# Small scale steps made assignable to GpSimd, and another order of all work, in a fused window-attention and gated-FFN kernel

## The chip, the core and the metric

The kernel runs on one core of one Trainium2 chip. The metric is the time of one execution in device microseconds (us). The engines are named as in the profile: PE (TensorE, with PEld for its weight loads), DVE (VectorE), ACT (ScalarE), POOL (GpSimd) and SP (SyncE, which here only issues DMAs).

## The reference

Window attention over 8 batches x 8 heads x 576 positions of head size 64, and then a gated feed-forward layer over the 4608 tokens:

```python
scores = q @ k.T / sqrt(64)                 # per batch and head
mask = (rel >= 0) & (rel < 64)              # rel = i - j: each row sees 64 keys
attn = softmax(where(mask, scores, -1e9))
x = (attn @ v) as 4608 x 512                # heads side by side
h = x @ w_in                                # 512 -> 2048
g = h * erf(softplus(h))
out = g @ w_out                             # 2048 -> 512
```

Inputs and output are float32; the two weight matrices arrive as float64.

## The kernel before

**Split numbers.** Every operand of a matrix product is split into two float16 parts, a high one and a rest, after scaling by a power of two; a product is then three float16 matmuls (high x high, high x rest, rest x high). So each tensor has a step that finds its peak, a short chain of scale steps on 128x1 to 128x4 values, a "high" step and a "rest" step.

**Attention** runs in 36 units of 128 tokens (u = 0..35). Per unit: peaks of q, k, v (`pk`), high and rest of q, k, v (`qh ql kh kl vh vl`), scores on PE (`s`), masked maximum on DVE (`m`), subtraction of the maximum (`f`), exponential on ACT (`e`), high and rest of the probabilities (`ec`, `r`), a transpose by DMA (`t`), the product with v on PE (`a`), and the division (`n`). Two units form a chunk of 256 tokens (c = 0..17). The result x of a chunk is split again (`xh`, `xl`) and transposed by DMA (`xt`, into tiles `xt`), two sets of which alternate.

**The weights** come in 16 pieces (`L:0` to `L:15`), are put together from float64 by integer steps (`d`, `c`, `o`), and get a scale per pair of pieces: `mb mx my` find the peak, `mc` gives the power of two and its inverse, `dg` puts the inverse on a diagonal matrix, `h` makes the high part and `lp le` or `l` the rest. `W`, `V`, `X` join the scales of pairs.

**The feed-forward part** runs in 36 passes: pass g takes half of the hidden features (g % 2) of one chunk (g // 2). The first four chunks use plain products (`mm`, 24 matmuls of 256 columns each; line 643), the others seven products of sums (`mw`, 24 matmuls of 128 columns; line 696), whose results are copied out of PSUM (`ew`) and added (`xw`). Then come softplus (`sp`), erf (`er`), the gate (`gt`), the high part (`gh`, tile gh) and the rest (`gl`, tile gl) for each half n of the pass, and the second product (`mA` with gh, 16 matmuls of 512 columns, `mB` with gl, 8; line 754). `fo` scales the result, `st` stores it. Softplus, erf and the exponential need different ACT tables, so each change between them loads one.

**What sets the order.** PLAN is a list of tokens `step:unit:part:engine`, where a, v or g as the last part puts the step on ACT, DVE or POOL. The program issues the steps in the list's order, and each engine runs its own steps in that order, whatever is ready. `wm:k:n` puts n matmuls without use on PE. Waits between engines follow from the tiles. Small helpers make the steps: `scaled` (lines 346 to 352) multiplies by a scale on the engine asked for, `narrow` (line 481 on ACT, 483 on DVE, 485 on POOL) converts, `inverse_pow2` (line 343) turns a power of two into its inverse, always on DVE.

```python
for tok in PLAN.split():
    name, *args = tok.split(":")
    HANDLERS[name](*(int(a) if a.isdigit() else a for a in args))
```

Of the kernel before, what the change touches and what calls it, by code (L numbers as in the profile page):

```python
# [19 lines left out]
W = 64  # L20
# [16 lines left out]
LOWEST = -3.0e38  # L37
EXP_BITS = 0x7F800000
# [204 lines left out]
def window_attention_gated_ffn(ctx, tc, q, k, v, w_in, w_out, masks, out):  # L243
# [98 lines left out]
    def inverse_pow2(dst, src, shift):  # L342
        nc.vector.tensor_scalar(dst.bitcast(I32), src.bitcast(I32), -1.0, float((254 + shift) * EXP_ONE),
                                op0=ALU.mult, op1=ALU.add)
# [221 lines left out]
    def pair_diag(j):  # L566
        nc.scalar.activation(diag[j % 2], unit, AF.Copy, scale=parts(2 * j)[1])
# [272 lines left out]
```

## Time and profile before

| | |
|---|---|
| time, median of 3 runs | 865.0 us (864.99 to 865.01) |
| the profiled execution's own time | 864.18 us |
| its span | 862.4 us |
| mean granted clock of PE | 0.992 |
| PE, PEld busy | 834.7 us (97%), 590.3 us (68%) |
| DVE, ACT, POOL busy | 713.8 us (83%), 648.3 us (75%), 315.3 us (37%) |
| ACT table loads | 115, 1283 ns each |

The span runs from the first to the last instruction; 1.8 us of the profiled execution lie around it. A matmul's busy time counts work without use (`wm`) like any other. Shares are means over the span, and the first 140 us look different from the rest.

### The profile page before, as it was taken

What the parts mean: (1) busy time and instruction counts of PE and PEld (TensorE: products, weight loads), DVE (VectorE), ACT (ScalarE), POOL (GpSimd) and SP (SyncE); (2) the same over time, 40 slices, a digit from 0 to 9 for tenths busy, and PEclk for the clock granted to TensorE, in tenths of its full rate; (3) what the DMA queues carried; (4) which work ended last, traced back from release to release, by engine and by line L of the source; (5) the groups of instructions that cost most, each with busy time, mean ns of one, the idle gap of its engine ahead of it and who ended that gap; (6) DMA issues with size and microseconds to landing.
All of it is one profiled execution on the core that took longest, in us unless ns stands there. A gap on an engine that the chain in (4) does not pass through costs nothing.

```text
span 862.4 us, 25961 instructions
## 1 busy us (share of the span) xinstructions
PE 834.7 (97%) x11042; PEld 590.3 (68%) x11042; DVE 713.8 (83%) x1587; ACT 648.3 (75%) x820; POOL 315.3 (37%) x272
## 2 busy tenths in 40 slices
PE   6889989999999999999999999999999999999997
PEld 4557666666667775967867768777777676776773
DVE  5989998999998889988888797988798989774342
ACT  5989999988976797888697686976676664644452
POOL 2325223332342443335164434633234464331110
PEclk8999999999999999999999999999999999999999
DMA  9976573444442474574646747545245362420000
GB/s 362 332 183 187 171 208 107 92 115 83 123 102 60 124 146 108 149 140 115 141 117 121 153 117 180 108 120 118 66 112 121 92 119 39 93 44 26 2 26 24
DMA packets 167236, 104.45 MB, mean 121 GB/s; under 512 B 139856, under 2 KB 144592, under 8 KB 167120
## 3 DMA queue, kind: packets, MB, share of 16 engines
q1 hardware_dynamic: 167120, 102.80, 47.9%
q8 instruction: 86, 1.41, 0.6%
q14 instruction: 30, 0.25, 0.1%
HBM read 54.72 MB, written 9.44 MB: 74 GB/s over the span
## 4 chain that ended last, share of the span: by engine, by line
PE 80%; ACT 8%; DVE 6%; DMA 4%; issue 1%; SPq 0%; ACTq 0%; DVEq 0%
PE o L754 40%; PE hp L696 29%; PE hp L643 5%; PE av L469 3%; PE s L434 2%; DMA w<-w_in 1%; DMA xt<-xs 1%; DVE sm L443 1%; ACT y L721 1%; ACT L725 1%; ACT y L725 1%; ACT h L481 1%; DMA stage<-w_out 1%; ACT L721 1%; PE o L589 1%
## 5 line engine op out<-in xcount | busy, mean ns | idle before, releaser
L754 PE MATMUL o<-w,gh 128*128 128x512 f16 x1152 | 260.5, 379 | 0.1
L754 PEld LDWEIGHTS <-gh 128*128 128x128 f16 x1152 | 109.5, 98 | 122.5 <-ACT gh L481 0.3
L696 PEld LDWEIGHTS <-w 128*128 128x128 f16 x2688 | 156.0, 98 | 15.3
L696 PE MATMUL hp<-xt,w 128*128 128x128 f16 x2688 | 164.3, 219 | 0.0
L754 PE MATMUL o<-w,gl 128*128 128x512 f16 x576 | 136.2, 379 | 0.0
L696 PE MATMUL hp<-xt,stage 128*128 128x128 f16 x2016 | 122.5, 219 | 1.1 <-DMA xt<-xs 0.8
L696 PEld LDWEIGHTS <-stage 128*128 128x128 f16 x2016 | 116.2, 98 | 10.7 <-issue 1.2
L721 ACT ACTIVATE y<-h,c 128x1024 f32<-128x1024 f32 x72 | 80.0, 1143 | 34.4 <-DVE h L483 33.9
L730 DVE SCALAR_TENSOR_TENSOR y<-h,cy,y 128x1024 f32<-128x1024 f32 x56 | 76.4, 1380 | 22.0 <-ACT y L725 21.5
L643 PE MATMUL hp<-xt,w 128*128 128x256 f16 x768 | 89.9, 276 | 3.6 <-DMA xt<-xs 1.8
L754 PEld LDWEIGHTS <-gl 128*128 128x128 f16 x576 | 53.3, 98 | 54.0 <-DVE gl L355 0.3
L481 ACT ACTIVATE h<-hp 128x512 f32<-128x512 f32 x88 | 51.4, 588 | 48.7 <-PE hp L696 42.6
L452 ACT ACTIVATE sm<-sm,shift,cde 128x512 f32<-128x512 f32 x72 | 57.3, 808 | 39.9 <-DVE sm L448 32.9
L643 PEld LDWEIGHTS <-w 128*128 128x128 f16 x768 | 74.5, 99 | 16.4 <-issue 4.9
L712 DVE TENSOR_TENSOR h<-hp,h 128x512 f32<-128x512 f32 x84 | 57.5, 685 | 33.1 <-PE hp L696 27.2
L725 ACT ACTIVATE y<-y 128x1024 f32<-128x1024 f32 x72 | 74.1, 1053 | 0.5
L448 POOL TENSOR_TENSOR sm<-sm,mx 128x512 f32<-128x512 f32 x37 | 47.5, 1290 | 61.7 <-DVE mx L443 61.5
L459 POOL TENSOR_TENSOR p<-sm,p 128x512 f16<-128x512 f32 x37 | 52.0, 1409 | 43.8 <-DVE p L483 30.2
L443 DVE CUSTOM_DVE_ANT_0 sm<-s,mask 128x128 f32<-128x128 f32 x288 | 65.2, 284 | 3.2 <-PE s L434 2.7
L744 POOL TENSOR_TENSOR gl<-y,gh 128x1024 f16<-128x1024 f32 x20 | 45.0, 2250 | 60.3 <-DVE gh L483 23.0
L721 ACT ACT_TABLE_LOAD x45 | 57.7, 1283 | 5.4 <-DVE gl L355 2.3
L483 DVE COPY h<-hp 128x512 f32<-128x512 f32 x56 | 38.3, 685 | 26.5 <-PE hp L696 24.4
(160 smaller groups left out, 1302.7 us busy)
## 6 DMA issues: line engine op xcount, KB each, us to landing
kr<-k_in SPq DMA_DIRECT2D x36, 384.0 KB, 3.5
qr<-q_in SPq DMA_DIRECT2D x36, 256.0 KB, 3.4
vr<-v_in SPq DMA_DIRECT2D x18, 512.0 KB, 4.2
out<-ob SPq DMA_DIRECT2D x36, 256.0 KB, 2.1
stage<-w_out SPq DMA_DIRECT2D x6, 1024.0 KB, 5.4
stage<-w_in SPq DMA_DIRECT2D x5, 1024.0 KB, 5.7
vs<-vs SPq DMA_DIRECT2D x36, 130.0 KB, 2.6
vr<-v_in SPq DMA_DIRECT2D x18, 256.0 KB, 3.1
```

Source lines behind the costliest of these rows:

```text
L443: nc.vector.tensor_tensor_reduce(smi(u, par)[:, j, :], sps[par][:, j, :], mask[:, var, :], 1.0, LOWEST, op0=ALU.add, op1=ALU.max, accum_ou ...
L448: eng_of(eng).tensor_tensor(s, s, m.unsqueeze(2).broadcast_to([P, HP, P]), op=ALU.subtract)
L452: nc.scalar.activation(s, s, AF.Exp, bias=shift14, scale=es)
L459: eng_of(eng).tensor_tensor(pp[1][u % 2][:, sl, :], smi(u, par), pp[0][u % 2][:, sl, :], op=ALU.subtract)
L481: nc.scalar.activation(dst, src, AF.Copy)
L643: nc.tensor.matmul(hps[pc % 2][:, f, :], w1[a][:, cc, fs], xt[b][c % 2][:, cc:cc + 5:4, :], start=(n == 0), stop=(n == 3 * NCC - 1))
L696: nc.tensor.matmul(dst, w, xt[b][c % 2][:, blk + cc, :], start=bool(first) and at + cc + a + b == 0, stop=at + cc + a == 3 * P + 2, skip_g ...
L712: nc.vector.tensor_tensor(dst, bank_of((1, 0, 1)[i]), dst, op=ALU.add)
L721: nc.scalar.activation(yat(g, n), at(hb, g, n), AF.Softplus, scale=st_c[g][:, n:n + 1])
L725: nc.scalar.activation(y, y, AF.Erf)
L730: nc.vector.scalar_tensor_tensor(y, at(hb, g, n), s, y, op0=ALU.mult, op1=ALU.mult)
L754: nc.tensor.matmul(ops[j], a[:, f, ts], w2[b][:, hf * GF + f, :], start=first and f == 0 and a is gh and b == 0, stop=last and f == GF - 1 ...
```

## The change

Four things change in the code. The short scale chains get an engine of their own in PLAN: the pair's inverse leaves `mc` and becomes `md`, two of the chunk's scale steps leave `pc` and become `pd`, and `W`, `V` and `X` take an engine. The diagonal `dg`, always on ACT before, takes an engine too. Maxima of two columns by `tensor_reduce` or `tensor_tensor` become one `tensor_scalar` (`larger`). And PLAN is another list: 2677 tokens in place of 2652, in another order, with other engines for many steps.

```diff
+HUGE = 2.0 ** 127
...
-    def inverse_pow2(dst, src, shift):
-        nc.vector.tensor_scalar(dst.bitcast(I32), src.bitcast(I32), -1.0, float((254 + shift) * EXP_ONE),
+    def inverse_pow2(dst, src, shift, eng="v"):
+        eng_of(eng).tensor_scalar(dst.bitcast(I32), src.bitcast(I32), -1.0, float((254 + shift) * EXP_ONE),
                                 op0=ALU.mult, op1=ALU.add)
...
     def chunk_scale(c):
         nc.vector.tensor_copy(cpw[c], call)
         inverse_pow2(csc[c], cpw[c], 14)
-        nc.vector.tensor_scalar(cde[c][:, 0:1], cpw[c][:, 2:3], 2.0 ** -14, None, op0=ALU.mult)
-        nc.vector.tensor_scalar(cde[c][:, 1:2], cpw[c][:, 0:1], cpw[c][:, 1:2], 2.0 ** -31, op0=ALU.mult, op1=ALU.mult)
+
+    def chunk_gain(c, eng):
+        e = eng_of(eng)
+        e.tensor_scalar(cde[c][:, 0:1], cpw[c][:, 2:3], 2.0 ** -14, 1.0, op0=ALU.mult, op1=ALU.mult)
+        e.tensor_scalar(cde[c][:, 1:2], cpw[c][:, 0:1], cpw[c][:, 1:2], 2.0 ** -31, op0=ALU.mult, op1=ALU.mult)
...
     def pair_scale(j):
-        kw, sw, i = (kw1, sw1, j) if j < 4 else (kw2, sw2, j - 4)
-        kw, sw = kw[:, i:i + 1], sw[:, i:i + 1]
-        exponent(kw, wall)
-        inverse_pow2(sw, kw, 12 if j < 4 else 14)
-
-    def pair_diag(j):
-        nc.scalar.activation(diag[j % 2], unit, AF.Copy, scale=parts(2 * j)[1])
+        exponent((kw1, kw2)[j // 4][:, j % 4:j % 4 + 1], wall)
+
+    def pair_gain(j, eng):
+        kw, sw = ((kw1, sw1), (kw2, sw2))[j // 4]
+        inverse_pow2(sw[:, j % 4:j % 4 + 1], kw[:, j % 4:j % 4 + 1], 14 if j // 4 else 12, eng)
+
+    def pair_diag(j, eng):
+        scaled(eng, diag[j % 2], unit, parts(2 * j)[1])
...
-    def w_in_scale(hf):
+    def larger(eng, dst, a, b):
+        eng_of(eng).tensor_scalar(dst, a, HUGE, b, op0=ALU.min, op1=ALU.max)
+
+    def w_in_scale(hf, eng):
         wm = wm1[:, hf:hf + 1]
-        nc.vector.tensor_reduce(wm, kw1[:, 2 * hf:2 * hf + 2], axis=AX.X, op=ALU.max)
-        inverse_pow2(isw[:, hf:hf + 1], wm, -10)
+        larger(eng, wm, kw1[:, 2 * hf:2 * hf + 1], kw1[:, 2 * hf + 1:2 * hf + 2])
+        inverse_pow2(isw[:, hf:hf + 1], wm, -10, eng)
...
```

PLAN is shown at three places by the order of the instructions on an engine (`hp_154` and `hp_155` are the two PSUM tiles of the products, `o_156` and `o_157` those of the result, other numbers tell buffers apart).

**POOL, from its first real work on** (`sw` is the pair's inverse, `tmp` the diagonal, `w_0` the high part of w_in, `c_88` and `cde` scales, `sm` the scores, `p_` probabilities). Before:

```order
L352 TENSOR_SCALAR w_0_136<-stage_148,sw_66 128x2x512
L352 TENSOR_SCALAR w_0_136<-stage_149,sw_66 128x2x512
L352 TENSOR_SCALAR w_0_136<-w_1_139,sw_66 128x2x512
L621 TENSOR_SCALAR c_88<-kw_65,cpw 128x2
L448 TENSOR_TENSOR sm_116<-sm_116,mx_92 128x512
```

and now:

```order
L354 TENSOR_SCALAR tmp<-tmp,sw_66 128x128
L354 TENSOR_SCALAR w_0_136<-stage_149,sw_66 128x2x512
L345 TENSOR_SCALAR sw_66<-kw_65 128x1
L354 TENSOR_SCALAR w_0_136<-w_1_139,sw_66 128x2x512
L354 TENSOR_SCALAR tmp<-tmp,sw_66 128x128
L405 TENSOR_SCALAR cde<-cpw 128x1
L406 TENSOR_SCALAR cde<-cpw 128x1
L453 TENSOR_TENSOR sm_116<-sm_116,mx_92 128x512
```

Two diagonals, the inverse of the second pair (L345) and the two chunk scales (L405, L406) have come to POOL, one high part has left it.

**PE, where chunk 2 begins** (`xt_1` is chunk 1's x, `xt_0` chunk 2's; `av` from `pt_1` is the attention product of unit 5, the last of chunk 2; `cmx` and `cdiag` belong to the scale of the next chunk). Before:

```order
L469 MATMUL av<-vs_115,pt_1_126 64x65
L643 LDWEIGHTS w_0_136
L643 MATMUL hp_155<-xt_1_133,w_0_136 128x256
...
L387 MATMUL av<-ident,cmx 128x128
L395 LDWEIGHTS ones
L395 MATMUL av<-cdiag,ones 128x3
L643 LDWEIGHTS w_0_136
L643 MATMUL hp_155<-xt_0_132,w_0_136 128x256
```

and now:

```order
L474 MATMUL av<-vs_115,pt_1_126 64x65
L652 LDWEIGHTS w_0_136
L652 MATMUL hp_155<-xt_1_133,w_0_136 128x256
...
L389 MATMUL av<-ident,cmx 128x128
L652 MATMUL hp_154<-xt_1_133,w_0_136 128x256
...
L397 MATMUL av<-cdiag,ones 128x3
L652 MATMUL hp_155<-xt_1_133,w_0_136 128x256
...
L439 MATMUL s_151<-ks_0_110,qs_0_106 64x128
...
L652 MATMUL hp_155<-xt_0_132,w_0_136 128x256
```

Between unit 5's last attention matmul and chunk 2's first product stood one plain product (24 matmuls); now three of them and the scores of unit 6 (48 small matmuls) stand there.

**ACT, the last passes** (`y` is softplus and erf in place, `h_141` pass 35's hidden values, `ob` the result). Before:

```order
L348 ACTIVATE ob_147<-o_157,sg 128x512
L721 ACT_TABLE_LOAD
L721 ACTIVATE y_143<-h_141,c_88 128x1024
L721 ACTIVATE y_144<-h_141,c_88 128x1024
L725 ACT_TABLE_LOAD
L725 ACTIVATE y_143<-y_143 128x1024
L725 ACTIVATE y_144<-y_144 128x1024
```

and now:

```order
L350 ACTIVATE ob_147<-o_157,sg 128x512
L730 ACT_TABLE_LOAD
L730 ACTIVATE y_143<-h_141,c_88 128x1024
L734 ACT_TABLE_LOAD
L734 ACTIVATE y_143<-y_143 128x1024
L730 ACT_TABLE_LOAD
L730 ACTIVATE y_144<-h_141,c_88 128x1024
L734 ACT_TABLE_LOAD
L734 ACTIVATE y_144<-y_144 128x1024
```

The halves of pass 35 go through softplus and erf one after the other, with four table loads in place of two. On PE, `mA:34:0` now stands ahead of the last two products of pass 35 (`mw:35:3`, `mw:35:4`), where it stood behind them; so three groups of line 754 (`mB:34:0`, `mA:34:1`, `mB:34:1`) in place of four lie between the last product and `mA:35:0`.

Over the whole program the same steps change engines like this (steps before, now): copies out of PSUM `ew` on ACT 62, 82 and on DVE 50, 30; peaks `pk` on ACT 60, 42 and on DVE 48, 66; `f` on POOL 37, 45; `gl` on POOL 20, 28; table loads in ACT's order 115, 131. The matmuls with use are the same in number; those without are 276 and now 275.

More of the change, by code (lines that the diff above doesn't have):

```diff
@@ L593, in low_out @@
         narrow(eng, parts(u)[3][:, a], ops[a])
-    def w_in_scale(hf):
+    def larger(eng, dst, a, b):
+        eng_of(eng).tensor_scalar(dst, a, HUGE, b, op0=ALU.min, op1=ALU.max)
+    def w_in_scale(hf, eng):
         wm = wm1[:, hf:hf + 1]
-        nc.vector.tensor_reduce(wm, kw1[:, 2 * hf:2 * hf + 2], axis=AX.X, op=ALU.max)
-        inverse_pow2(isw[:, hf:hf + 1], wm, -10)
-    def w_out_scale(hf):
-        m, r = pm[:, hf:hf + 1], pr[:, hf:hf + 1]
-        pair = slice(2 * hf, 2 * hf + 2)
-        nc.vector.tensor_reduce(m, kw2[:, pair], axis=AX.X, op=ALU.max)
-        inverse_pow2(r, m, 0)
-        nc.vector.tensor_scalar(rw2[:, pair], kw2[:, pair], r, None, op0=ALU.mult)
-        nc.vector.tensor_scalar(kwo[:, hf:hf + 1], m, 2.0 ** -4, None, op0=ALU.mult)
@@ L608, in joint_scale @@
-    def joint_scale():
-        m, r, w, iw, ko = (all1[:, i:i + 1] for i in range(5))
-        nc.vector.tensor_tensor(m, pm[:, 0:1], pm[:, 1:2], op=ALU.max)
-        nc.vector.tensor_tensor(w, wm1[:, 0:1], wm1[:, 1:2], op=ALU.max)
-        inverse_pow2(r, m, 0)
-        inverse_pow2(iw, w, -10)
-        nc.vector.tensor_scalar(all4, kw2, r, None, op0=ALU.mult)
-        nc.vector.tensor_scalar(ko, m, w, 2.0 ** -4, op0=ALU.mult, op1=ALU.mult)
-        nc.vector.tensor_tensor(st_y, kw1, all4, op=ALU.mult)
-        nc.vector.tensor_scalar(st_y, st_y, iw, 2.0 ** -10, op0=ALU.mult, op1=ALU.mult)
+        larger(eng, wm, kw1[:, 2 * hf:2 * hf + 1], kw1[:, 2 * hf + 1:2 * hf + 2])
@@ new lines, in w_in_scale, with w_out_scale, joint_scale @@
+        inverse_pow2(isw[:, hf:hf + 1], wm, -10, eng)
+    def w_out_scale(hf, eng):
+        e, m, r = eng_of(eng), pm[:, hf:hf + 1], pr[:, hf:hf + 1]
+        larger(eng, m, kw2[:, 2 * hf:2 * hf + 1], kw2[:, 2 * hf + 1:2 * hf + 2])
+        inverse_pow2(r, m, 0, eng)
+        e.tensor_scalar(rw2[:, 2 * hf:2 * hf + 2], kw2[:, 2 * hf:2 * hf + 2], r, 1.0, op0=ALU.mult, op1=ALU.mult)
+        e.tensor_scalar(kwo[:, hf:hf + 1], m, 2.0 ** -4, 1.0, op0=ALU.mult, op1=ALU.mult)
+    def joint_scale(eng):
+        e = eng_of(eng)
+        m, r, w, iw, ko = (all1[:, i:i + 1] for i in range(5))
+        larger(eng, m, pm[:, 0:1], pm[:, 1:2])
+        larger(eng, w, wm1[:, 0:1], wm1[:, 1:2])
+        inverse_pow2(r, m, 0, eng)
+        inverse_pow2(iw, w, -10, eng)
+        e.tensor_scalar(all4, kw2, r, 1.0, op0=ALU.mult, op1=ALU.mult)
+        e.tensor_scalar(ko, m, w, 2.0 ** -4, op0=ALU.mult, op1=ALU.mult)
+        e.tensor_tensor(st_y, kw1, all4, op=ALU.mult)
+        e.tensor_scalar(st_y, st_y, iw, 2.0 ** -10, op0=ALU.mult, op1=ALU.mult)
@@ L776, in window_attention_gated_ffn @@
     HANDLERS = {
-        "lm": load_mask, "lq": load_q, "lk": load_k, "lv": load_v, "pk": peak, "pa": chunk_max, "pb": chunk_rows, "px": chunk_top, "py": chunk_all, "pc": chunk_scale,
+        "lm": load_mask, "lq": load_q, "lk": load_k, "lv": load_v, "pk": peak, "pa": chunk_max, "pb": chunk_rows, "px": chunk_top, "py": chunk_all, "pc": chunk_scale, "pd": chunk_gain,
         "qh": q_hi, "ql": q_lo, "kh": k_hi, "kl": k_lo, "vh": v_hi, "vl": v_lo, "vc": v_copy, "s": scores, "m": masked_max,
@@ L780, in window_attention_gated_ffn @@
         "xt": x_turn, "L": fetch, "d": low_bits, "c": rebias, "o": assemble,
-        "b": bound, "dg": pair_diag, "lp": low_sum, "le": low_out, "mb": pair_rows, "mx": pair_top, "my": pair_all, "mc": pair_scale, "h": high, "l": low,
+        "b": bound, "dg": pair_diag, "lp": low_sum, "le": low_out, "mb": pair_rows, "mx": pair_top, "my": pair_all, "mc": pair_scale, "md": pair_gain, "h": high, "l": low,
         "W": w_in_scale, "V": w_out_scale, "X": joint_scale, "dc": descale, "gn": gains, "mm": mm1, "ev": hidden, "mw": product, "ew": take, "xw": add, "xd": x_sums, "S": w_sums,
```

379 rows, old and new, of the table PLAN are left out of this document.

## The prediction

> **What bounds the kernel now.** I read the page first (busy time by engine, the chain that ended last), then the busy times by stretch, then the timelines at the places where PE stood idle. The page:
>
> ```profile
> span 862.4 us, 25961 instructions
> PE 834.7 (97%) x11042; PEld 590.3 (68%) x11042; DVE 713.8 (83%) x1587; ACT 648.3 (75%) x820; POOL 315.3 (37%) x272
> PE 80%; ACT 8%; DVE 6%; DMA 4%; issue 1%; SPq 0%; ACTq 0%; DVEq 0%
> ```
>
> PE is the bound: 97% busy, and 80% of the last chain. The stretches (columns: busy us of PE, PEld, DVE, ACT, POOL with counts, then PE's granted clock and two DMA columns) say how much each is worth:
>
> ```profile
> 0.00:58.78 58.78, 42.61 (x528) 28.55 (x529) 46.48 (x117) 46.74 (x73) 17.54 (x31) 0.91 0.86 286
> 58.78:104.40 45.62, 44.01 (x580) 32.67 (x580) 43.78 (x117) 44.52 (x57) 16.39 (x16) 1.00 0.70 209
> 104.40:129.06 24.66, 20.55 (x254) 16.82 (x254) 23.91 (x57) 23.68 (x39) 7.84 (x7) 1.00 0.72 193
> 129.06:136.00 6.94, 6.94 (x48) 5.34 (x48) 6.37 (x8) 6.19 (x10) 0.00 (x0) 0.76 0.45 139
> 136.00:250.00 114.00, 113.96 (x1223) 74.17 (x1222) 107.36 (x249) 106.35 (x136) 44.43 (x36) 1.00 0.41 103
> 250.00:837.00 587.00, 585.76 (x8317) 423.38 (x8316) 479.33 (x1037) 413.35 (x501) 226.95 (x181) 1.00 0.45 102
> ```
>
> From 136 to 837 us PE misses 1.28 us in all. There an order can win nothing and only lose: the matmuls are the same. What can be won lies ahead of 136 us, where DVE and ACT are busy to 96 and 97% (58.78 to 129.06: 67.69 and 68.20 of 70.28 us) and PE waits for them. The largest hole there is at the change from chunk 1 to chunk 2. PE's timeline, with two rows of chunk 1's beginning first:
>
> ```profile
> 97.16 0.86 PE L434 MATMUL s<-ks,qs 64*64 64x128 f16 x48
> 97.96 5.41 PE L643 MATMUL hp<-xt,w 128*128 128x256 f16 x48
> ...
> 121.27 0.95 PE L469 MATMUL av<-vs,pt 128*64 128x65 f16 x48
> 123.77 2.78 PE L643 MATMUL hp<-xt,w 128*128 128x256 f16 x24 [1.55 <-ACT h L481]
> 127.60 0.16 PE L395 MATMUL av<-cdiag,ones 128*128 128x3 bf16 x1 [1.00 <-DVE cdiag L392]
> 129.06 7.12 PE L643 MATMUL hp<-xt,w 128*128 128x256 f16 x48 [1.29 <-DMA xt<-xs]
> ```
>
> The brackets are idle time and what ended it: 1.55 + 1.00 + 1.29 = 3.84 us. The 48 matmuls behind it took 7.12 us where as many took 5.41 us at 97.96; the granted clock from 129.06 to 136 is 0.76. So the hole costs 3.84 + 1.71 = 5.55 us.
>
> **The change, part by part.** (1) *Chunk 2 begins later in PE's order.* Behind the last attention matmul of unit 5 (end 121.27 + 0.95 = 122.22 us) runs division, narrowing, rest and DMA transpose; chunk 2's first product starts at 129.06. These rows, of DVE and of ACT, are steps of that chain:
>
> ```profile
> 123.47 0.69 DVE L477 TENSOR_TENSOR x<-av,rd 128x512 f32<-128x512 f32 x1
> 125.29 0.69 DVE L504 TENSOR_TENSOR xs<-x,xs 128x512 f16<-128x512 f32 x1
> 124.20 0.63 ACT L481 ACTIVATE xs<-x 128x512 f16<-128x512 f32 x1
> ```
>
> The chain needs 129.06 - 122.22 = 6.84 us. Before, PE had one product of 24 matmuls to cover it (2.7 us, half of 5.41); now it has three and a score step, 3 x 2.7 + 0.8 = 8.9 us (the scores at 97.16 last 0.8 us to the next start). The cover exceeds the chain by 2.1 us. If nothing else holds PE there, the hole closes: -5.55 us, which is the lower end. The upper end is 0: the wait could be for ACT, not for the order (first rival).
>
> (2) *Chunk 1 begins as before, but one of its rests moves to POOL.* Between unit 3's attention and chunk 1's first product PE has the same work in both lists. Before, that product (97.96) followed the scores without idle time. The rest of x, by engine:
>
> ```profile
> L504 POOL TENSOR_TENSOR xs<-x,xs 128x512 f16<-128x512 f32 x8 | 12.1, 1510 | 33.4 <-ACT xs L481 21.6 <-DVE xs L483 11.8
> L504 DVE TENSOR_TENSOR xs<-x,xs 128x512 f16<-128x512 f32 x14 | 11.0, 784 | 0.2
> ```
>
> The rest of unit 3 takes 1510 ns on POOL in place of 784 on DVE. Nothing shows slack, so I take the whole +0.73 us; ends 0 and 0.73.
>
> (3) *Scale steps on POOL.* On DVE an inverse takes 154 ns. POOL's nearest row is its scale of 128x2, here by minimum, median and maximum:
>
> ```profile
> L343 DVE TENSOR_SCALAR sw<-kw 128x1 int32<-128x1 int32 x8 | 1.2, 154 | 0.3
> L621 POOL TENSOR_SCALAR c<-kw,cpw x29: 266/269/2207, 27.0 to 707.1; 128x2 f32<-128x2 f32 x29
> L621 POOL TENSOR_SCALAR c<-kw,cpw 128x2 f32<-128x2 f32 x29 | 18.4, 639 | 44.6 <-DVE cpw L398 44.6
> 52.72 1.27 ACT L348 ACTIVATE w<-stage,sw 128x1024 f16<-128x1024 f32 x1 [1.00 <-DVE sw L343]
> 21.05 2.09 POOL L352 TENSOR_SCALAR w<-w,sw 128x1024 f16<-128x1024 f32 x1 [2.15 <-DVE sw L343]
> 24.40 1.28 DVE L355 SCALAR_TENSOR_TENSOR w<-w,sw,w 128x1024 f16<-128x1024 f32 x1
> ```
>
> So a moved inverse is later by 0.11 to 2.05 us, by the mean 639 ns by 0.49. For the second pair there is room: its high part on POOL (21.05) ended at 23.14 and the DVE step that reads it came at 24.40, 1.26 us later. Chunk scales are wanted only by the exponential, behind scores and maximum, and gains by results much later. The place without cover is the fourth pair: ACT already waits there (1.00 us until the inverse), and now its diagonal and high part follow an inverse on POOL. Queued behind ACT's wait are narrowings and the high parts of chunk 1, which PE wants. I take +0.5 us, the mean; ends 0.1 and 2.05. [...]
>
> (4) *The end.* Rows of PE, ACT, DVE and POOL:
>
> ```profile
> 837.03 3.62 PE L754 MATMUL o<-w,gh 128*128 128x512 f16 x16
> 840.49 1.89 PE L754 MATMUL o<-w,gl 128*128 128x512 f16 x8
> 842.22 3.62 PE L754 MATMUL o<-w,gh 128*128 128x512 f16 x16
> 845.67 1.89 PE L754 MATMUL o<-w,gl 128*128 128x512 f16 x8
> 847.39 3.62 PE L754 MATMUL o<-w,gh 128*128 128x512 f16 x16
> 838.01 1.28 ACT L721 ACT_TABLE_LOAD   x1 [1.42 <-DVE h L483]
> 839.30 2.19 ACT L721 ACTIVATE y<-h,c 128x1024 f32<-128x1024 f32 x2
> 842.80 2.01 ACT L725 ACTIVATE y<-y 128x1024 f32<-128x1024 f32 x2
> 834.75 0.68 DVE L712 TENSOR_TENSOR h<-hp,h 128x512 f32<-128x512 f32 x1
> 837.24 0.69 DVE L483 COPY h<-hp 128x512 f32<-128x512 f32 x1
> 843.89 2.48 DVE L730 SCALAR_TENSOR_TENSOR y<-h,cy,y 128x1024 f32<-128x1024 f32 x2 [5.96 <-ACT y L725]
> 846.29 0.68 DVE L483 CAST gh<-y 128x1024 f16<-128x1024 f32 x1
> 830.65 2.92 POOL L485 TENSOR_SCALAR gh<-y 128x1024 f16<-128x1024 f32 x2 [12.47 <-DVE y L730]
> ```
>
> Before, the last product ended at 837.03, gh was there at 846.97, and PE reached it only at 847.39: no wait. Now, from the last product on: 0.2 to the copy, 0.69 copy, 0.68 addition (now behind it), 0.1 hop, 1.28 table, 1.10 softplus of one half, 1.28 table, 1.01 erf, 1.24 gate, 0.68 gh: 8.26 us. PE's three groups last 1.73 + 3.45 + 1.72 = 6.90 us (starts above). It waits 1.36 us. The second half needs from 6.34 (first erf done) 1.28 + 1.10 + 1.28 + 1.01 + 1.24 + 1.46 (gh on POOL, half of 2.92) = 13.71, and PE is free at 8.26 + 3.45 + 1.73 = 13.44: 0.27 more. I take +1.6 us. Ends: 0.9 if the addition runs ahead of the copy, 2.3 if POOL's step is held as long as the 128x2 ones (0.7 more).
>
> (5) *What I cost at nothing.* Sixteen more table loads, copies moved from DVE to ACT and rests moved from DVE to POOL lie mostly beyond 250 us:
>
> ```profile
> L744 POOL TENSOR_TENSOR gl<-y,gh 128x1024 f16<-128x1024 f32 x20 | 45.0, 2250 | 60.3 <-DVE gh L483 23.0 <-ACT gh L481 18.9 <-PE hp L696 10.7
> ```
>
> 16 x 1.28 = 20.5 us of loads on ACT (838.01) stand against 587 - 413 = 174 us in which it idles there, eight rests of 2250 ns = 18 us on POOL against 587 - 227 = 360 us. PE covers them as long as the gap between a pass's last product and its `mA` stays near what it was. In PE's order that gap is shorter than 11 us for passes 11, 12 and 15 now, and was for 11, 33 and 35; only in pass 35 does it fall below 10. If that cover were gone, each late pass would cost PE about 1 us. The one matmul without use that is gone (276 to 275), and the different gaps that these fill, cost nothing: PE waits there anyway. The loads at the start stand in another order (a v and a weight piece ahead of two k), but the first four weight pieces, which set the pace, keep their places.
>
> **The sum.** -5.55 + 0.73 + 0.5 + 1.6 = -2.7 us. The profiled execution took 864.18 us (862.4 span and 1.8 around it), 0.8 below the median of 865.0, so both move alike: **862.3 us**. Ends of the terms: -5.55 + 0 + 0.1 + 0.9 = -4.55, so 860.4; with part (1) at half (-2.8) and the others as taken it is 865.0. Less than 0.2% (1.7 us) can hardly be told from no change here.
>
> **Rivals.** *ACT still sets the pace, no change.* ACT is busy 23.68 of 24.66 us ahead of chunk 2. In its queue ahead of chunk 2's first product stand 137 steps in place of 142, by the means of their kinds 0.9 us less. PE has meanwhile one score step (0.8) more done. If ACT decides, the hole shrinks by 1.7 us only, and 1.6 + 0.5 go back: about 865.4 us. For it: the first wait of the hole (1.55) was ended by ACT. Against: the other two were ended by DVE and the transpose, and DVE has some 4.8 us less ahead of that point. *Slower: POOL's scale steps are held.* Inverses of the second, third and fourth pair and their diagonals stand in series with ACT's and POOL's high parts in the first 60 us. At 2.05 us for each of three, 6.2 in place of 0.5, the time is 862.3 + 5.7 = 868.0; it comes out slower than before from 1.5 us each on. For it: one of the POOL rows reaches 2207 ns. Against: the median is 269. *Faster than forecast.* The scores of unit 2 now stand ahead of the first product, so if that product starts no later than 58.78, PE is 0.8 us of work ahead, and DVE, with 4.6 us less queued ahead of it by the means, may start it up to 2 us earlier: 862.3 - 2.8 = 859.5.
>
> **Chances.** Forecast 0.53, no change 0.22, held POOL 0.15, faster still 0.10. The forecast case alone spans 860.4 to 863.3; a part of it, 0.02, falls within 0.2%. With the rivals the range is 859.0 to 866.8, which leaves out the held case and the tip of the fast one. Faster by over 0.2%: 0.51 + 0.10 = 0.61; within 0.2%: 0.22 + 0.02 = 0.24; slower: 0.15.
>
> **What would show it.** Right: PE has no hole of more than 1 us between unit 5's attention and chunk 2, the clock stays at 1.00 there, PE waits about 1.4 us for gh of pass 35, and up to 0.7 us for the transposed x of chunk 1. Wrong: the hole is still there with ACT as its releaser; or new waits of PE between 136 and 837 us add up to more than 2 us, which would mean that the order has lost its slack in the middle.

## The result, and the profile after

The changed kernel takes 876.95 us (median of 4 runs, 876.41 to 877.73) where the kernel before took 865.0 (864.59 to 865.01): a ratio of 1.014, 95% interval 1.0122 to 1.0158. It is slower by 12 us, and the forecast said 862.3. The profiled execution took 877.49 us with a span of 875.7. The lines of its page that answer to those of before:

```profile
span 875.7 us, 25858 instructions
PE 838.9 (96%) x11041; PEld 591.4 (68%) x11041; DVE 705.3 (81%) x1567; ACT 666.3 (76%) x811; POOL 337.9 (39%) x299
PE 66%; DVE 10%; DMA 5%; ACT 5%; issue 2%; SPq 1%; POOL 1%; DVEq 0%; ACTq 0%; POOLq 0%
```

PE's share of the last chain fell from 80 to 66%. The same stretches as in the prediction, and one from 250 to 850 us (columns: PE, PEld, DVE, ACT, POOL busy, PE's clock, two DMA columns):

```profile
0.00:58.78 58.78, 43.11 (x521) 29.26 (x522) 43.79 (x104) 45.15 (x70) 18.50 (x37) 0.88 0.87 282
58.78:104.40 45.62, 42.04 (x512) 29.69 (x511) 42.34 (x112) 43.94 (x57) 16.32 (x18) 1.00 0.78 209
104.40:129.06 24.66, 24.16 (x331) 19.79 (x329) 23.11 (x57) 23.98 (x35) 10.13 (x11) 1.00 0.80 192
129.06:136.00 6.94, 5.16 (x87) 4.14 (x85) 6.94 (x22) 6.56 (x11) 0.60 (x1) 1.00 0.38 90
136.00:250.00 114.00, 112.93 (x1196) 74.61 (x1194) 105.29 (x225) 102.44 (x125) 46.30 (x46) 1.00 0.42 105
250.00:850.00 600.00, 590.33 (x8277) 423.35 (x8275) 478.52 (x1046) 435.24 (x511) 239.37 (x184) 1.00 0.48 101
```

From 250 to 850 us PE now misses 9.67 us; before it missed 1.24 from 250 to 837. PE's waits beyond 130 us, by what ended them (us in total, times, longest); these are the first six of eleven rows, the others are of 0.5 us and less. Before, this list had one row of 0.8 us:

```profile
PE av L474 <- DMA pt<-p: 4.1, 2, 3.4
PE hp L705 <- DVE h L488: 1.8, 2, 0.9
PE hp L652 <- DMA xt<-xs: 1.5, 1, 1.5
PE s L439 <- issue: 1.4, 1, 1.4
PE av L389 <- DVE cmx L342: 1.2, 3, 0.6
PE hp L705 <- DVE h L721: 0.6, 2, 0.3
```

To see where the time went I laid PE's two programs beside each other: the start of a group of matmuls less the PE work that its own list puts ahead of it (2.69 us a plain product, 1.34 a product of sums, 3.45 and 1.73 the second products, 0.80 scores, 0.51 half an attention product). How much later that is than before, at the group named:

| group | starts at, us | later than before, us |
|---|---|---|
| `s:0` | 30.0 | -1.5 |
| `a:1:1` (unit 1, attention) | 52.8 | +1.8 |
| `mA:0:0` | 91.2 | +2.8 |
| `a:5:1` | 120.6 | +4.3 |
| `mA:1:0` | 143.7 | +1.0 |
| `mA:9:0` | 296.8 | +1.8 |
| `mA:9:1` | 310.2 | +2.4 |
| `mA:10:0` | 325.9 | +7.4 |
| `mA:15:0` | 438.0 | +8.3 |
| `mA:16:0` | 461.3 | +10.5 |
| `mA:20:0` | 558.3 | +12.2 |
| `mA:23:0` | 618.5 | +13.2 |
| `mA:34:0` | 847.3 | +13.0 |
| end | 871.3 | +13.4 |

So the hole at chunk 2 did shrink (from +4.3 to +1.0), but 4.3 us had been lost ahead of it, and over 11 us were lost between 297 and 620 us, in single places. Each row compares two single executions. That of the old order with nothing but the new code (below) stands +1.2 at `a:5:1`, +1.8 at `mA:1:0` and +1.7 at the end by the same measure. So a difference of under 2 us ahead of 145 us is not shown by it, while the loss behind is: from `mA:2:0` to the end that execution moves by 0.1 us. The largest of these places is unit 12's attention. PE, then SP's queue (a SP row's duration is the issue alone):

```profile
317.40 1.29 PE L474 MATMUL av<-vs,pt 128*64 128x65 f16 x44 [3.36 <-DMA pt<-p]
305.02 1.24 SPq L467 DMA_TRANSPOSE pt<-p  x1
308.66 0.33 SPq L363 DMA_DIRECT2D kr<-k_in  x1
309.09 0.64 SPq L429 DMA_DIRECT2D vs<-vs  x1
309.78 0.59 SPq L430 DMA_DIRECT2D vs<-vs  x1
310.47 1.69 SPq L467 DMA_TRANSPOSE pt<-p  x1
```

and the rest of the probabilities on POOL that the second transpose reads, with the DVE step that the load of k waits for (it frees k's buffer):

```profile
305.04 1.16 POOL L464 TENSOR_TENSOR p<-sm,p 128x512 f16<-128x512 f32 x1 [3.89 <-DVE p L488]
307.62 1.02 DVE L357 SCALAR_TENSOR_TENSOR ks<-kr,csc,ks 128x768 f16<-128x768 f32 x1
```

The data were ready at 306.2, but in SP's list the load of k for unit 17 and the copy of v for unit 13 stood between unit 12's two transposes. SP stood at the load until 308.64, issued the transpose at 310.47, and it landed 6.9 us later, the longest of the 72 transposes of probabilities:

```profile
DMA to landing us min/median/max: 3.0/3.3/6.9
```

PE's mean granted clock was 0.72 over six us from 316 on (second row), so that 5.0 us were lost in all:

```profile
310.00:316.00 6.00, 4.04 (x28) 1.85 (x25) 4.59 (x8) 5.70 (x9) 1.16 (x1) 1.00 1.19 142
316.00:322.00 6.00, 4.60 (x117) 4.31 (x118) 3.20 (x6) 2.73 (x4) 1.15 (x1) 0.72 0.69 183
```

Over the whole program 53 of the 144 transposes landed later than 4 us after their issue, 31 before (from each issue and the last of its landing events in the trace). The load and the two copies issued ahead of the transpose at 310.47 landed at 313.6, 315.2 and 315.5, that transpose at 317.4, and none of the 341 DMAs on SP landed ahead of one issued earlier, before or now. That this order is what made it late is not shown by it.

### The profile page after: what moved, and what is told of

Read it like the earlier page. It is cut to its first block, busy times and chain, and to the rows that moved or that the text cites. A ratio compares the mean times of both kernels' runs of the same rounds, so it can differ in the third digit from the quotient of the medians.

```text
span 875.7 us, 25858 instructions
## 1 busy us (share of the span) xinstructions
PE 838.9 (96%) x11041; PEld 591.4 (68%) x11041; DVE 705.3 (81%) x1567; ACT 666.3 (76%) x811; POOL 337.9 (39%) x299
## 3 DMA queue, kind: packets, MB, share of 16 engines
q8 instruction: 86, 1.41, 0.7%
## 4 chain that ended last, share of the span: by engine, by line
PE 66%; DVE 10%; DMA 5%; ACT 5%; issue 2%; SPq 1%; POOL 1%; DVEq 0%; ACTq 0%; POOLq 0%
PE o L763 34%; PE hp L705 24%; PE hp L652 4%; PE av L474 3%; PE s L439 2%; DMA pt<-p 2%; ACT y L730 1%; DVE sm L448 1%; DVE y L739 1%; ACT L730 1%; DVE vs L357 1%; DMA kr<-k_in 1%; DMA stage<-w_out 1%; DVE h L721 1%; ACT L734 1%
## 5 line engine op out<-in xcount | busy, mean ns | idle before, releaser
L753 POOL TENSOR_TENSOR gl<-y,gh 128x1024 f16<-128x1024 f32 x28 | 64.0, 2289 | 106.6 <-DVE gh L488 51.7
L486 ACT ACTIVATE h<-hp 128x512 f32<-128x512 f32 x106 | 61.5, 586 | 51.9 <-PE hp L705 47.8
L453 POOL TENSOR_TENSOR sm<-sm,mx 128x512 f32<-128x512 f32 x45 | 56.0, 1249 | 94.4 <-DVE mx L448 94.3
L739 DVE SCALAR_TENSOR_TENSOR y<-h,cy,y 128x1024 f32<-128x1024 f32 x56 | 74.1, 1326 | 20.2 <-ACT y L734 20.2
L464 POOL TENSOR_TENSOR p<-sm,p 128x512 f16<-128x512 f32 x34 | 44.6, 1318 | 51.3 <-DVE p L488 27.0
```

Of the source, the lines that this page charges most:

```text
L453: eng_of(eng).tensor_tensor(s, s, m.unsqueeze(2).broadcast_to([P, HP, P]), op=ALU.subtract)
L486: nc.scalar.activation(dst, src, AF.Copy)
L739: nc.vector.scalar_tensor_tensor(y, at(hb, g, n), s, y, op0=ALU.mult, op1=ALU.mult)
L753: eng_of(eng).tensor_tensor(glb[:, sl], yat(g, n), ghb[:, sl], op=ALU.subtract)
```

## The experiments

Ratios are to runs of the kernel before on the same chip, with 95% intervals.

**Whose loss: the scale steps or the order.** First the changed order with POOL's small steps undone:

```diff
-md:1:g dg:0:g pd:0:g W:0:g V:0:g ...   (15 steps of md, pd, dg, W, V on POOL, and one dg on DVE)
+md:1:v dg:0:a pd:0:v W:0:v V:0:v ...
```

> The changed kernel with its order, but every inverse (md), chunk scale (pd) and W, V, X back on DVE and every diagonal back on ACT. Theory A (the 12 us are lost by the order: transposes that land late behind loads, and single waits for evacuations): 877 us, within 1 us of the changed kernel, with the waits at 317, 459 and 553 us still there. Rival B (the small POOL steps are held and hold others): 872 us or less, and fewer waits beyond 250 us.

873.72 us (872.64 to 876.9), ratio 1.0108 (1.008 to 1.0136). PE still waited at 317 (1.69 us), 369, 430, 457 and 549 us, and the head was no better (`mA:0:0` +2.9). Between `mA:9:0` and `mA:10:0`, where that first wait lies, it lost 2.7 us and the changed kernel 5.6; the two profiles differ by 3.6 in all. That is neither A's 877 nor B's 872 without waits; the kernel with the repairs, below, takes this up again.

Then the other side, the order of before with the POOL steps, and with nothing but the new code (same list, `md` behind `mc` and `pd` behind `pc` on DVE):

> The order of the kernel before, in the code of the changed one, with the same small scale steps and diagonals on POOL as the changed kernel has them. Theory A (the order loses the time): 865 us, within 1 us of the kernel before. Rival B (POOL's small steps lose it): 868 us or more.

> The order of the kernel before in the code of the changed one, each small scale step on DVE and each diagonal on ACT as before. If the code of the helpers costs nothing: 864.7 us, within 0.5 us of the kernel before, so that the 1.6 us of the run with the POOL steps belong to POOL. If the 1.6 us come from the helpers: 866 us.

With POOL steps 866.27 us, 1.0018 (1.0007 to 1.003); with the code alone 865.09, 1.0000 (0.9985 to 1.0015). So POOL's steps cost the old order 1.2 to 1.6 us by the medians, though the two intervals overlap. One place shows it: PE waits 2.15 us for a pair's peak where it waited 1.06 before and with the code alone.

```profile
79.83 0.16 PE L563 MATMUL av<-wtop,ones 1*128 1x1 bf16 x1 [2.15 <-DVE wtop L560]
```

**The transpose at 317 us.**

```diff
-t:12:0 ... kl:15 mw:11:2 pd:7:v lk:17 m:13:1 vc:13 er:10:0 mw:11:6 f:13:0:v t:12:1
+t:12:0 ... kl:15 mw:11:2 pd:7:v m:13:1 er:10:0 mw:11:6 f:13:0:v t:12:1 lk:17 vc:13
```

> The changed kernel with one edit in SP's order: the load of k for unit 17 and the copy of v for unit 13 (three DMAs) go behind the transpose of unit 12's second probabilities instead of ahead of it. Theory A (the transpose is held in SP's queue behind a load that waits for a buffer, and then lands behind what was issued ahead of it): it is issued near 306.3 in place of 310.47 and lands within 4 us, PE's wait of 3.36 us at 317 us goes, and with it the lost clock of that stretch (0.83 over 10 us, 1.7 us): 872.3 us, between 871.5 and 874. Rival C (ACT's table loads between maximum and exponential, and DVE's queue, make unit 12 and 13 late anyway): 876 us or more, with a wait at the same place under another releaser.

872.33 us (871.84 to 873.26), 1.0086 (1.0071 to 1.0101). SP issued both transposes from 305.47 on, and PE no longer waited for unit 12:

```profile
305.47 2.62 SPq L467 DMA_TRANSPOSE pt<-p  x2
314.23 0.95 PE L474 MATMUL av<-vs,pt 128*64 128x65 f16 x48
320.70 0.25 PE L474 MATMUL av<-vs,pt 128*64 128x65 f16 x4 [0.21 <-DMA pt<-p]
321.87 0.89 PE L474 MATMUL av<-vs,pt 128*64 128x65 f16 x44 [0.92 <-DMA pt<-p]
```

Moving three DMAs in a list gives back 4.6 us. A new wait of 1.13 us (0.21 and 0.92) appeared at unit 13, whose transposes stand behind two loads of q; C holds for that much.

**Does the middle lose on its own?** Before's order up to `mA:1:0`, then the changed one:

> The order of the kernel before up to the second product of pass 1 (143 us), with its scale steps on DVE and ACT, then the order of the changed kernel. Theory A (the middle loses its 12 us at places of its own): 876 to 878 us. Rival D (the middle only suffers because the head of the changed kernel leaves the engines late): 870 us or less.

875.49 us (872.33 to 877.24), 1.0117 (1.0091 to 1.0144): half a microsecond under A's bounds, far from D's. In its profile PE loses 9.5 us more than before from `mA:9:0` on (11.6 in the changed kernel). The middle loses its time whatever stands ahead of it; D falls.

**DMA order in the head.**

```diff
-r:0:0:g vc:1 mx:2 ... lk:3 d:9 ... t:0:0 ... t:0:1
+r:0:0:g mx:2 ... d:9 ... t:0:0 ... t:0:1 vc:1 lk:3
-t:3:1 ... t:3:0 ... n:2 h:11:g vc:3
+vc:3 t:3:1 ... t:3:0 ... n:2 h:11:g
-pc:2 L:12 gl:0:0 kh:4:g xt:2:0 ... xt:2:1 qh:5:a kl:4 vh:4:a lq:6 ... xt:3:1
+pc:2 gl:0:0 kh:4:g xt:2:0 ... xt:2:1 L:12 qh:5:a kl:4 vh:4:a ... xt:3:1 lq:6
```

> The kernel of the 305 us edit, with three more edits in SP's order, all ahead of 104 us: unit 1's copy of v and unit 3's load of k go behind the two transposes of unit 0; unit 3's copy of v goes ahead of its last transpose; the load of weight piece 12 and of unit 6's q go behind the transposes of chunk 1's x that they stood ahead of. Theory A (transposes and copies land late for what SP issues ahead of them): PE's 3.19 us at 47 us shrinks to below 1, the 1.4 us at 90 us and the 0.8 us at 102 us go, and 2 to 4 us remain of that at the end: 868.3 to 870.3 us. Rival E (ahead of 136 us ACT and DVE, busy to 95% there, set the pace, so the waits only change their releasers): 872 us.

877.56 us, 1.0152 (1.012 to 1.0184): a miss of A and of E. The first two edits did a part of what A said: `a:1:1` came 1.5 us sooner than in the kernel of the 317 us edit, `mA:0:0` 1.6, and the wait at 90 us went, but at 46 us PE still waited 1.44 us for unit 0's transposes. And the load of weight piece 12, moved behind two transposes, came too late for ACT, which waited 5.32 us for it; behind that piece its queue holds pass 1's softplus and the copy that PE waited for:

```profile
105.50 4.73 PE L652 MATMUL hp<-xt,w 128*128 128x256 f16 x22 [5.95 <-ACT h L486]
```

**The wait with no releaser.** `s:27` moved from ahead of `mw:21:3` to behind it.

> The kernel of the 305 us edit, with the scores of unit 27 one product later on PE (24 matmuls between them and unit 25's attention product). The wait of 1.21 us with no releaser stood at the same instruction of PE in four kernels, 14017 instructions from the start, and a second one 1024 later. Theory F (PE's own instructions arrive late: they come in pieces of 16 KB, one of which started at 546.9 us, and the stretch of small matmuls ahead uses them up faster than the others): the wait shrinks to below 0.4 us, 871.3 us. Rival G (it comes from the transfers of that time, whatever PE runs): the wait stays above 0.8 us, 872.3 us.

872.94 us (870.45 to 873.21), 1.0091. The total doesn't tell it apart from 872.33, the place does. What was won there was lost again at the peak rows of chunk 15 (614 us), where PE waited 1.53 us in place of 0.51. The changed kernel, then this one:

```profile
552.72 0.25 PE L439 MATMUL s<-ks,qs 64*64 64x128 f16 x4 [1.37 <-issue]
```

```profile
549.34 0.58 PE L439 MATMUL s<-ks,qs 64*64 64x128 f16 x28 [0.26 <-issue]
```

F's condition (below 0.4) is met here, and in the three later kernels with this move it was 0.23 us or less; F's 871.3 us is not.

**Six local repairs at once, then without the one that failed.**

```diff
 vc:1 lk:3, vc:3, lk:17 vc:13 and s:27 as above; L:12 and lq:6 left alone
-ew:17:2:a pb:11 mA:16:0          # both pb moves only in the first of the two kernels
+ew:17:2:a mA:16:0 pb:11
-e:29:1 pb:15 mA:23:0
+e:29:1 mA:23:0 pb:15
-ec:13:0:a r:13:1:g lq:17 ... t:13:1          # lq:16 lq:17 only in the second
+ec:13:0:a r:13:1:g ... t:13:1 lq:16 lq:17
```

> The changed kernel with six local moves: the 305 us edit; unit 1's copy of v and unit 3's load of k behind unit 0's transposes; unit 3's copy of v ahead of its last transpose; the scores of unit 27 one product later; the peak rows of chunks 11 and 15 (a matmul of 128x128 that waits for a DVE maximum) behind the first second product of passes 16 and 23 instead of ahead of it. Weight piece 12 and unit 6's q stay where the changed kernel has them. Theory A with F (single late arrivals at known places, each worth its wait): against the 872.3 us of the 305 us edit, -1.5 at 47 us, -0.2 at 90 us, -0.9 at 549 us, -0.4 at 457 us and -0.7 at 614 us: 868.6 us, between 867 and 870.5. Rival C (the engines behind are late anyway, so that each wait comes back a little later): 871.5 us or more.

> The kernel of the six repairs without the move of the peak rows of chunks 11 and 15, and with the two loads of q ahead of unit 13's transposes behind them. Theory A: the 1.6 and 1.3 us that came behind the moved peak rows are gone (0.4 and 0.7 come back ahead of them), and the wait of 1.2 us at 320 us goes: 870.3 us, between 869 and 871.5. Rival C (what one wait gives is taken by the next): 872 us or more.

The first took 873.15 us, 1.009 (1.0065 to 1.0116), so A's 867 to 870.5 is missed and C's bound of 871.5 reached. At pass 2 it stood 1.95 us ahead of the 317 us edit (the second kernel, with the same list up to there, 0.6), but behind the moved peak rows PE waited for what hangs on them (0.56 us each for the next step of that chain, and more behind): from `mA:16:0` to `mA:17:0` it lost 1.6 us, from `mA:23:0` to `mA:24:0` 1.4. The second took 870.95 us (869.87 to 872.13), 1.0072 (1.0058 to 1.0085), inside A's bounds, but not in all as A said: the wait at unit 13 stayed at 0.84 us with the loads of q behind, so these were not what held it. What PE still waits for beyond 250 us there:

```profile
PE hp L705 <- DVE h L488: 1.8, 2, 0.9
PE av L474 <- DMA pt<-p: 1.5, 2, 0.8
PE av L389 <- DVE cmx L342: 1.5, 3, 0.8
PE hp L705 <- DVE h L721: 0.8, 2, 0.4
PE s L439 <- issue: 0.2, 1, 0.2
```

5.8 us in sum, and 870.95 is 6.3 above 864.63. In the two waits of 0.9 a product needs a PSUM bank whose copy stands on DVE straight behind a gate; the first of them (PE went on at 367.21):

```profile
364.40 2.16 DVE L739 SCALAR_TENSOR_TENSOR y<-h,cy,y 128x1024 f32<-128x1024 f32 x1
366.48 0.68 DVE L488 COPY h<-hp 128x512 f32<-128x512 f32 x1
```

The scale steps once more, where that wait at 317 us is repaired (edit of the first run on this kernel):

> The kernel with the repairs but without the moved peak rows (870.95 us, ratio 1.0072), and in it the 16 small steps that stood on POOL back on DVE and ACT. Theory A (the order loses the time, and the 3 us that the first run without POOL steps won came from its one wait at 317 us, whose transposes happened to land 1.7 us sooner): nothing is left to win there, 870.5 us, ratio 1.006 to 1.008. Rival B (POOL's small steps cost 3 us wherever they stand): 868 us, ratio 1.004 or less.

873.0 us (871.27 to 875.47), 1.0094 (1.0078 to 1.011). Nothing is won; the median is 2 us higher, which A did not say either, and the intervals overlap. Rival B falls for this order. That the first run's 3 us were mostly its one wait fits both runs.

**Does closing the hole at chunk 2 win?** Before's order with a piece of the changed one in it, in three cuts:

| | from before | changed order | then before's |
|---|---|---|---|
| first | up to `mA:0:0` | up to `mA:1:0` | rest |
| second | up to `mA:0:0` | up to `mA:2:1` | rest |
| third | - | up to `mB:2:1`, with the repairs of the head | rest |

> The order of the kernel before up to the first second product of pass 0 (88 us), then that of the changed kernel up to the first second product of pass 1 (143 us), then that of the kernel before; scale steps on DVE and ACT in the first and last part. It puts the changed order at the change from chunk 1 to chunk 2 alone into the kernel before. Theory H (three products and a score step behind unit 5's attention cover the chain of chunk 2, and the hole of 3.84 us with its lost clock closes to 1.5 us as in the changed kernel): 861.5 us, between 860.5 and 862.5. Rival I (ACT's queue sets that point, or the seams cost as much): 865 us or more.

> As the kernel that has the changed order from 88 to 143 us alone, but the changed order holds 23 us longer, up to the second half of pass 2 (166 us), where by the means of their kinds no engine has more queued ahead of PE's work than in the kernel before; at the earlier seam DVE had 2.2 us more, and PE waited 1.09 us there for a rest on DVE and 0.94 us for unit 6's transposes. Theory H (the hole at chunk 2 closes by 2.0 us, and only the seam gave it back): 862.6 us, between 861.8 and 863.4. Rival I (what is won at chunk 2 is lost to later waits wherever the seam is): 864.2 us or more.

> The changed order up to pass 2's last second product (166 us), with the repairs ahead of 104 us that held (copies and one load of k behind unit 0's transposes, unit 3's copy of v ahead of its last one), then the order of the kernel before. In the run of the six repairs PE stood 0.7 us better at pass 2 than in the kernel before. Theory A (head and middle add up): 864.0 us, between 863 and 865, and no waits like those of the changed kernel beyond 250 us. Rival J (ahead of 170 us DVE and ACT set the pace, so that PE's gains there are paid back at the seam): 864.8 us or more. If a part of the 12 us beyond 250 us came from the changed head: 868 us or more.

864.18 us, 0.9998 (0.9983 to 1.0013); 864.01 us, 0.9995 (0.9984 to 1.0007); 864.98 us, 1.0005 (0.9994 to 1.0015). By the measure of the table the hole shrank by 3.0 to 3.3 us each time (from `a:5:1` to `mA:1:0`), and within 40 us PE had lost 2.1 to 2.4 us again. Rows of the second kernel:

```profile
130.37 5.30 PE L652 MATMUL hp<-xt,w 128*128 128x256 f16 x47 [1.60 <-DMA xt<-xs]
168.62 0.23 PE L389 MATMUL av<-ident,cmx 128*128 128x128 bf16 x1 [0.69 <-DVE cmx L342]
171.98 0.16 PE L397 MATMUL av<-cdiag,ones 128*128 128x3 bf16 x1 [1.40 <-DVE cdiag L394]
```

By the measure of the table, PE stood 2.0 us ahead of before at `mA:1:0` in the first, 1.2 and 2.7 at `mA:2:0` in the other two; one pass on it was 0.0 behind, 1.2 behind and 0.5 ahead. H's 861.5 and 862.6 us did not come; I's bounds of 865 and 864.2 are missed by 0.8 and 0.2 us. The third time lies within A's range and above J's bound, so it doesn't part those two. None of the three beats the kernel before by what can be told. And no wait like those of the changed kernel stood beyond 250 us in any of them (the longest is 0.68 us), the third with the changed head included, so the loss in the middle belongs to the order there.

## Why the prediction was wrong

**The step that failed is part (5), "what I cost at nothing".** It said that PE covers the middle "as long as the gap between a pass's last product and its `mA` stays near what it was". That gap did hold: no row of PE's waits beyond 130 us names gh, and none names ACT. So no wait of PE ended with the 16 table loads or the copies on ACT; whether they made the chains behind its waits later was not tested. But it is one chain of four. The others were never laid beside PE's work: probabilities through SP's queue to attention (4.1 us of waits and 1.7 of clock), a product behind the copy or addition that frees its bank (2.4), the peak rows (the small matmul that waits for DVE's maximum) that stand in PE's order ahead of a big product (1.2), and waits without a releaser (1.7): 11.1 of the 11.6 us. The order of DMAs on SP was not read in the middle at all, though in SP's list the pair `t:12:0 t:12:1` stood together before, and three DMAs between now. The text named what would show this ("new waits of PE between 136 and 837 us add up to more than 2 us"); it gave the case no chance of its own, and the slower rival with 0.15 was another mechanism.

**Part (1), -5.55 us: mechanism seen, end not.** At that place 3.3 us came back (+4.3 to +1.0): waits of 0.29 and 1.48 in place of 3.84 us, and the clock stayed at 1.00.

```profile
120.15 0.95 PE L474 MATMUL av<-vs,pt 128*64 128x65 f16 x48
129.93 0.75 PE L439 MATMUL s<-ks,qs 64*64 64x128 f16 x40 [0.29 <-DVE qs L357]
132.38 5.30 PE L652 MATMUL hp<-xt,w 128*128 128x256 f16 x47 [1.48 <-DMA xt<-xs]
124.88 1.28 DVE L509 TENSOR_TENSOR xs<-x,xs 128x512 f16<-128x512 f32 x2
125.59 3.82 SPq L513 DMA_TRANSPOSE xt<-xs  x3
```

The chain that I took as 6.84 us long needed 132.38 - 121.10 = 11.3 here: DVE makes the rests of units 4 and 5 one after the other, so three transposes queue on SP for 3.82 us, behind two loads of 1 MB. The length of a chain is a property of the order too. And 4.3 us had been lost earlier, 3.3 of them between `s:0` and `a:1:1`, where at 47 us PE waited for unit 0's transposes, which landed behind a load and two copies of v and a load of k:

```profile
47.23 0.25 PE L474 MATMUL av<-vs,pt 128*64 128x65 f16 x4 [3.19 <-DMA pt<-p]
```

No term of the sum looks at the DMAs of that stretch. The three cuts fit one reading of the head: ahead of 170 us DVE and ACT have the work (93 and 97% busy from 58.78 to 129.06, rows above), and what PE gains at one wait it gives back at the next. No run changes their work, so this is argued, not shown. It makes the rival "ACT still sets the pace, no change", at 0.22, the nearer one for the head, though its hole was to shrink by 1.7 us only and DVE is the later releaser.

**Part (2), +0.73:** chunk 1 cost more, and only a little of it for POOL's rest. PE waited 1.39 us for the copy of v that the list puts behind unit 3's transposes on SP, and 0.82 for xt. The transpose of POOL's rest was issued as that rest ended and landed 0.46 us behind the one that ended the 0.82; PE waited 0.10 more for it:

```profile
89.71 0.57 PE L474 MATMUL av<-vs,pt 128*64 128x65 f16 x24 [1.39 <-DMA vs<-vs]
101.92 2.29 PE L652 MATMUL hp<-xt,w 128*128 128x256 f16 x17 [0.82 <-DMA xt<-xs]
```

**Part (3), +0.5, and the rival "held".** POOL's inverses took 190, 242 and 621 ns (minimum, median, maximum), far from 2207. One of the three diagonals took 1835 ns, the others 372 and 373. What made single steps on POOL this long (2207 before) no run shows. In the old order the steps cost 1.2 to 1.6 us, within the ends that I gave; in the new one nothing that shows. So the longest length that part (3) allowed for an inverse did not come. That rival also had a sum wrong: at 1.5 us each it gives 866.3 us, and it is slower than 865.0 from 1.1 us each on.

**Part (4), +1.6:** it was 0.4. `mA:35:0` came 2.03 us after the group ahead of it, which takes 1.73 (0.30 lost), the second half lost 0.1. The mis-sized term is the table load: I put 1.28 us of it behind the addition, but here it stands ahead of the waiting step and ran during the wait. In the kernel before it had come behind the wait (838.01, among the prediction's rows); why the two differ is open.

```profile
846.89 1.28 ACT L730 ACT_TABLE_LOAD   x1
854.98 1.15 ACT L730 ACTIVATE y<-h,c 128x1024 f32<-128x1024 f32 x1 [6.81 <-DVE h L721]
858.63 1.89 PE L763 MATMUL o<-w,gl 128*128 128x512 f16 x8
860.66 3.63 PE L763 MATMUL o<-w,gh 128*128 128x512 f16 x16
```

What stays open: 5.8 us of single waits in the best repaired kernel, which were found but not each undone, and why the same transpose at 317 us landed after 6.9, 5.2 and 4.3 us in three kernels with the same DMAs ahead of it.

## What to carry to other kernels

Where an order covers everything, it can only lose, and it loses at every chain, so each chain that ends at the bound engine has to be laid beside it: also the DMA queue, whose list was here an order of landing as well as of issue (none of 341 DMAs landed ahead of one issued earlier). Keep a transpose that the bound engine waits for ahead of loads that wait for a buffer (4.6 us given back here); but a load moved back has its own reader (5.95 us lost for one). And a wait that went away in a stretch where other engines are full was worth nothing in three cuts (ratios of 0.9995 to 1.0005).

## What the runs showed of the hardware

**PE stood without a releaser at a fixed instruction.** The wait stood at the same instruction of PE, 14017 from the start, in the five kernels with the changed order there (0.85 to 1.37 us), and in some a second one 1024 further. The page has 86 instruction transfers of 1.41 MB together, 16 KB each:

```profile
q8 instruction: 86, 1.41, 0.7%
```

One of them started at 550.3 us, a microsecond ahead of the wait, while the DMA engines were 86% busy (545 to 560 us) and behind a stretch of 48 + 48 + 72 + 48 + 44 small matmuls. In the run with the scale steps put back on the repaired kernel the second one took 1.29 us. In all twelve such waits at these two places, over eight kernels and from 0.23 us on, PE went on 1.25 to 1.52 us after a transfer of 16 KB of instructions had ended. So late instructions are what fits; why those transfers came no sooner is open.

**The clock falls or doesn't after the same wait.** Same place, same list there; the first kernel (six repairs) waited 1.69 us and kept its clock, the second (without the peak rows) waited 1.45 and lost 1.67 us on the same 47 matmuls:

```profile
130.89 5.31 PE L652 MATMUL hp<-xt,w 128*128 128x256 f16 x47 [1.69 <-DMA xt<-xs]
```

```profile
130.60 6.97 PE L652 MATMUL hp<-xt,w 128*128 128x256 f16 x47 [1.45 <-DMA xt<-xs]
131.00:136.00 5.00, 5.00 (x34) 3.89 (x33) 3.41 (x18) 2.98 (x7) 2.04 (x2) 0.69 0.01 2
```

So the clock fell behind a wait of 1.45 us once, and not behind one of 1.69 another time. In the trace's clock record the fall here, the one at 317 us in the changed kernel and the one at chunk 2 before are each a stretch of 3.41 us at 0.50, so 1.71 us lost. A term for the clock, as the 1.71 us in part (1), is a chance and not a sum.
